# Fewer and planned unread products at the start, value loads on a second DMA queue, and operands read into other places

## The chip, the cores and the metric

The kernel runs on one core of a Trainium2 chip. A core has five engines with a program each: TensorE (PE, matrix products), VectorE (DVE), ScalarE (ACT), GpSimd (POOL) and SyncE (SP), which in this kernel only issues DMA. They wait for one another through semaphores. The metric is the device time of one execution in microseconds (us); lower is better.

## The reference

Attention in chunks of 32 rows, each of which looks at 8 memory keys and at the keys from 16 rows before the chunk to 8 rows after it (64 in all), and then two feed-forward layers of 512 by 2048, all in float32:

```python
for c in range(nc):                       # 24 chunks of 32, 4 batches x 8 heads, head_dim 64
    q_c = q[:, :, c_start:c_end]
    k_full = np.concatenate([mem_k, k[:, :, l_start:r_end]], axis=2)
    v_full = np.concatenate([mem_v, v[:, :, l_start:r_end]], axis=2)
    scores = scale * np.matmul(q_c, k_full.transpose(0, 1, 3, 2))
    a = np.exp(scores - np.max(scores, axis=-1, keepdims=True))
    a = a / (np.sum(a, axis=-1, keepdims=True) + 1e-09)
    out[:, :, c_start:c_end] = np.matmul(a, v_full)
...
h = x @ w_in                              # x: 3072 x 512, w_in: 512 x 2048
g = h * np.clip(h + 3.0, 0.0, 6.0) / 6.0
x = g @ w_out                             # 2048 x 512
...
h = x @ w_in2
x = np.maximum(0.01 * h, h) @ w_out2
```

## The kernel before, in words

**The products.** Nearly all of the work is the four large matrix products. They run on TensorE in a float32 form of reduced precision, with each operand split into a high and a low part; a product of one 128-wide slice of the hidden layer with 512 rows is 12 matmuls of 128x512 (`h<-xh,w` eight times and `h<-xl,w` four times at L998, and `y<-g,w` twelve times at L1047). Later blocks of rows go in pairs, by a scheme with seven products in place of eight (L1322, L1490), whose sums of operands and results are made on ACT, DVE and POOL (`x_pair` reads the operands, L1126; L341 and L344 are the helpers that record copies, casts and two-operand operations, whatever they are for).

**The weights** arrive as 64-bit words (L393, 512 KB each, 32 per layer), are turned into float32 by ACT (L396) and DVE (L400, L404, L408), and are then split into their two parts (L341, L344).

**The attention** is cut into units. The first two (`unit(0, 0)` and `unit(0, 1)`, with the PSUM banks `at` and `ab`) and two half units (banks `h` and `ac`) come before any product; the others are threaded between the products. A unit loads queries and keys (`qk`), copies keys into windows (L341 on ACT, DVE or POOL), makes scores on PE (L544; L811 for half units), takes maxima (DVE, L561), exponentials (ACT, L568 and L580; L845), sums and norms (L594, L598), transposes on PE (L602; L866), copies the transposed rows back (`take_p`, ACT L341), multiplies with the values on PE (L622 and L634; L882) and hands rows on as operand `xh`, `xl` of the products or to the DRAM tensor `attended`. The values of a unit come in two tiles of six DMAs each: L502 four times (56x3x128, 84 KB) and L504 twice (8x6x128), all on SP's queue. Up to the unit whose scores start at 201 us they land in places of the pool `w`; the values, queries and keys of the four later units, and the operands `x` of the pairs, lie in places of the smaller pool `a`.

**The order.** Nobody wrote the order of instructions by hand. Every step is a task with an engine, a cost in ns and what it depends on, and `schedule` (a list scheduler with a model of DMA lanes, of the instruction queue of PE and of buffers) writes each engine's program from them; the engines then run their programs strictly in order. A change of any cost, and any new task, can therefore reorder all five programs.

**The unread products.** `warm` adds tasks that multiply the identity `ident` with itself into a bank that nobody reads (L461). They stand at fixed places: ahead of the first scores and behind each of the following steps of the four early units, first 512 columns wide, later 256. A float32 matmul of this kind, as those of the attention, is two instructions on PE in the trace: `x48` in the order is `x96` in the trace. The transposes are one each.

## Time and profile before

| | |
|---|---|
| median of 3 runs | 1046.41 us (1045.3 to 1048.34) |
| profiled execution | 1046.62 us |
| its span, from the first to the last instruction | 1044.8 us |
| PE busy | 1029.5 us, 99% of the span |
| DVE, ACT, POOL busy | 856.0, 694.8 and 23.9 us |
| mean granted TensorE clock | 0.998 |
| chain that ended last | PE 85%, DMA 6%, DVE 4%, ACT 2% |

The profiled execution is 0.2 us above the median, and 1.8 us of it lie outside the span. Times in rows are microseconds from the span's start. In a row of the timeline, "x17" is the number of instructions merged into it, and what stands in brackets is how long the engine had been idle before it and what ended that; "issue" is a wait for nothing that the profile shows.

### The profile page before, as it was taken

The numbers are of one execution on the slowest core, as the hardware profiler recorded it, in microseconds if no ns is written. First come the engines' busy times: TensorE is split into PE (matmuls) and PEld (weight loads), VectorE is DVE, ScalarE is ACT, GpSimd is POOL, SyncE is SP. The second block draws the span as 40 slices with busy tenths as digits, with TensorE's granted clock in tenths as the row PEclk, the third lists the DMA queues.
The fourth block names the chain that finished last, engine by engine and source line by source line (L and its number), as shares of the span: only waits on it lengthen the run. The fifth ranks groups of instructions, "written<-read, shape, count | busy, mean of one in ns | idle before, by whom it ended". The sixth has DMA issues, their size and how long they took to land.

```text
span 1044.8 us, 20156 instructions
## 1 busy us (share of the span) xinstructions
PE 1029.5 (99%) x7476; PEld 846.7 (81%) x7476; DVE 856.0 (82%) x1422; ACT 694.8 (67%) x1478; POOL 23.9 (2%) x31
## 2 busy tenths in 40 slices
PE   7999999999999999999999999999999999999998
PEld 4788888877888888888888888888888888888887
DVE  6995897578998778699999898999476998566775
ACT  4886776555988554576786576776565874666753
POOL 3010000000000000000000000000000000000000
PEclk9999999999999999999999999999999999999999
DMA  9989787776888888664647884446342554432451
GB/s 259 298 237 323 256 286 236 247 256 215 276 288 292 292 279 278 245 217 127 212 135 268 291 286 162 147 158 218 117 167 81 177 194 153 169 114 95 148 181 61
DMA packets 127315, 220.50 MB, mean 211 GB/s; under 512 B 12528, under 2 KB 76016, under 8 KB 127216
## 3 DMA queue, kind: packets, MB, share of 16 engines
q1 hardware_dynamic: 127216, 219.20, 63.2%
q8 instruction: 59, 0.97, 0.4%
q14 instruction: 40, 0.33, 0.1%
HBM read 156.24 MB, written 62.91 MB: 210 GB/s over the span
## 4 chain that ended last, share of the span: by engine, by line
PE 85%; DMA 6%; DVE 4%; ACT 2%; SPq 2%; issue 1%; DVEq 0%; ACTq 0%
PE y L1322 17%; PE y L1490 12%; PE h L1322 11%; PE y L1047 10%; PE h L1490 8%; PE hx L1322 8%; PE hx L1490 8%; PE h L998 3%; PE h L1047 2%; DMA w<-in_raw 2%; DMA kept1i<-ys 1%; DMA a<-in_raw 1%; PE at L634 1%; DMA half<-ys 1%; PE at L544 1%
## 5 line engine op out<-in xcount | busy, mean ns | idle before, releaser
L344 DVE TENSOR_TENSOR w<-w 128x512 fp32r<-128x512 f32 (+2 forms) x393 | 323.3, 858 | 29.0 <-ACT w L341 28.4
L341 ACT CAST w<-w 128x512 fp32r<-128x512 f32 (+1 forms) x290 | 223.7, 805 | 12.5 <-DMA w<-floats 3.9
L1047 PE MATMUL y<-g,w 128*128 128x512 f32 (+1 forms) x540 | 124.9, 375 | 1.5 <-ACT g L341 0.6
L1322 PE MATMUL y<-w 128*128 128x512 f32 x516 | 124.2, 389 | 0.0
L1322 PEld LDWEIGHTS y<-w 128*128 128x128 f32 x516 | 96.7, 188 | 20.1
L1047 PEld LDWEIGHTS y<-g,w 128*128 128x128 f32 x540 | 94.0, 188 | 19.9 <-ACT g L341 1.4
L1490 PE MATMUL y<-w 128*128 128x512 f32 x384 | 90.3, 389 | 0.0
L341 ACT CAST g<-w 128x512 fp32r<-128x512 f32 x80 | 49.7, 623 | 58.3 <-PE y L1490 22.5
L1490 PEld LDWEIGHTS y<-w 128*128 128x128 f32 x384 | 72.1, 188 | 15.0
L1296 ACT ACTIVATE w<-w 128x512 f32<-128x512 f32 x72 | 45.3, 633 | 43.9 <-DVE w L1289 21.5
L998 PE MATMUL h<-xh,w 128*128 128x512 f32 (+1 forms) x288 | 66.0, 370 | 0.0
L344 DVE TENSOR_TENSOR g<-w,g 128x512 fp32r<-128x512 f32 x80 | 54.4, 689 | 11.5 <-ACT g L341 11.4
L1490 PE MATMUL h<-w 128*128 128x512 f32 x264 | 62.1, 389 | 0.0
L1322 PE MATMUL h<-xl,w 128*128 128x512 f32 x240 | 58.3, 391 | 1.2 <-ACT xl L341 1.2
L1490 PE MATMUL hx<-w 128*128 128x512 f32 x252 | 59.2, 389 | 0.0
L1490 PEld LDWEIGHTS h<-w 128*128 128x128 f32 x264 | 49.5, 188 | 10.3
L998 PEld LDWEIGHTS h<-xh,w 128*128 128x128 f32 x288 | 49.7, 188 | 9.0
L1490 PEld LDWEIGHTS hx<-w 128*128 128x128 f32 x252 | 47.3, 188 | 9.8
L1322 PEld LDWEIGHTS h<-xl,w 128*128 128x128 f32 x240 | 44.8, 188 | 11.3 <-ACT xl L341 1.6
L1322 PE MATMUL y<-xh,w 128*128 128x512 f32 x216 | 51.9, 389 | 0.0
L1367 DVE TENSOR_TENSOR w<-y,w 128x512 f32<-128x512 f32 x35 | 23.9, 687 | 29.9 <-PE y L1322 27.1
L1322 PEld LDWEIGHTS y<-xh,w 128*128 128x128 f32 x216 | 40.5, 188 | 8.5
(242 smaller groups left out, 1847.7 us busy)
## 6 DMA issues: line engine op xcount, KB each, us to landing
w<-kept2i SPq DMA_DIRECT2D x42, 512.0 KB
w<-kept2o SPq DMA_DIRECT2D x42, 512.0 KB
w<-kept1i SPq DMA_DIRECT2D x28, 512.0 KB
a<-in_raw SPq DMA_DIRECT2D x20, 448.0 KB
w<-in_w1i SPq DMA_DIRECT2D x16, 512.0 KB
w<-in_w1o SPq DMA_DIRECT2D x16, 512.0 KB
w<-in_w2i SPq DMA_DIRECT2D x16, 512.0 KB
w<-in_w2o SPq DMA_DIRECT2D x16, 512.0 KB
```

Of the source, the lines that this page charges most:

```text
L341: nc.scalar.copy(out, in_) if e == "ACT" else engine(e).tensor_copy(out=out, in_=in_)
L344: engine(e).tensor_tensor(out=out, in0=a, in1=b, op=ALU.subtract)
L544: nc.tensor.matmul(ps.t[h * CHUNK:(h + 1) * CHUNK, par, i * W:(i + 1) * W], qk[h // 2].t[r, gp, (h % 2) * G + c * CHUNK:(h % 2) * G + (c + ...
L634: nc.tensor.matmul(pv.t[(h % 2) * D:(h % 2 + 1) * D, par, (h // 2) * 2 * G + i * CHUNK:(h // 2) * 2 * G + (i + 1) * CHUNK], v[h // 2].t[r, ...
L998: nc.tensor.matmul(h.t[:, o:o + n], w.t[:, 1 if p == 1 else 0, k * 128:(k + 1) * 128], x[:, k, c0:c0 + n], start=(p == 0 and k == 0 and o ...
L1047: nc.tensor.matmul(bank(banks[d])[:, c0:c0 + n], w.t[:, 1 if p == 1 else 0, d * 128:(d + 1) * 128], g.t[:, 1 if p == 2 else 0, at:at + n], ...
L1296: return add(lambda e: nc.scalar.activation(out=at(), in_=at(), func=AF.Prelu, alpha=0.01), {"ACT": act(N)}, key, after=[after], uses=uses)
L1322: nc.tensor.matmul(bank(to), wt(l, o)[:, kt * 128:(kt + 1) * 128].bitcast(F32R), operand(p, name, 1 if q == 2 else 0, kt).bitcast(F32R), s ...
L1367: done[2] = add(lambda e: nc.vector.tensor_tensor(out=half_of(x, 0), in0=bank(bb), in1=ut.t[:, 0], op=ALU.add), low, key, after=[k, done[1 ...
L1490: nc.tensor.matmul(bank(to[d]), wt(1 if q == 1 else 0, o)[:, d * 128:(d + 1) * 128].bitcast(F32R), g.t[:, 1 if q == 2 else 0], start=(fres ...
```

## The change

1. `warm` and its fixed places are gone. `schedule` itself puts in an unread product (`filler`, L483 in the changed kernel) wherever it finds PE without a task before the first large product, as long as a bank is open for it (`opens` and `closes` on the attention's steps say when): 128 columns wide before the first scores, 256 after.
2. The values of units 4 and later (`by_pool`) are issued by GpSimd's queue, 96 DMAs in eight units, 12 a unit; the loads ahead of them stay on SP.
3. Weights 2 to 23 get a `hold`: GpSimd copies one element of the weight two before, once that has landed, into the new weight's place, and the load waits for that copy. So at most two of these loads are under way.
4. The operands of the first pair (`x_pair`, p < -1) are read into places of `w`, not of `a`.
5. The windows of the second early unit are copied by ACT and not by DVE.
6. Costs and due times of the planner: cheaper value loads, another model of when a load has landed and of the instruction queue of PE, no safety margin before 20 us.

```diff
-STARTS, LANDS, SURE = 1900.0, 500.0, 1500.0
-HELD, FETCHED, FETCH, STALL = 447, 256, 5000.0, 250.0
+STARTS, LANDS, SURE, SOONER, MOST = 1900.0, 250.0, (0.0, 1500.0), 20000.0, 8000.0
+HELD, FETCHED, ASKS, FETCH, STALL = 447, 256, (256, 400), 2500.0, 250.0
+FIRST, LATER, FIRST_TILL = (128, 430.0), (256, 450.0), 3800.0
...
                 if pick is None:
+                    if e == "PE" and not progress and spots and (begun or now < FIRST_TILL):
+                        cols, took = LATER if begun else FIRST
+                        filler(spots[0], cols)
...
                     continue
...
+        if hold:
+            before, landed = hold
+
+            def follow(e):
+                nc.gpsimd.tensor_copy(out=make(t, ([128, 512, 2], U32))[:1, 0, :1].bitcast(F32), in_=before.t[:1, 0, :1].bitcast(F32))
+
+            k = add(follow, {"POOL": 100.0}, early, after=[*after, landed], allocs=[t], uses=[before])
+            k = add(load, {"SP": dma(524288, 380.0)}, early, after=[k], uses=[t])
...
+        by_pool = j >= 4 and not plain
...
-                        nc.sync.dma_start(out=v[i].t[par * D + NMEM:(par + 1) * D, g], in_=there)
+                        (nc.gpsimd if by_pool else nc.sync).dma_start(out=v[i].t[par * D + NMEM:(par + 1) * D, g], in_=there)
...
-        t = [add(windows(i), ({"DVE": 850.0} if i or quad else {"ACT": 1050.0}) if j == 0 else {"ACT": 1050.0}, key - 30, after=[l1[i]], allocs=[kw[i]], uses=[qk[i]]) for i in range(2)]
+        t = [add(windows(i), ({"DVE": 850.0} if i and not quad else {"ACT": 1050.0}) if j == 0 else {"ACT": 1050.0}, key - 30, after=[l1[i]], allocs=[kw[i]], uses=[qk[i]]) for i in range(2)]
...
-        src = {n: Buf("a") for n in ("b11", "b12", "b21", "b22")}
+        src = {n: Buf("w" if p < -1 else "a") for n in ("b11", "b12", "b21", "b22")}
...
-    warm(2)
-    warm(1, marks["s", 0, 0])
-    warm(2, marks["s", 0, 1])
...
-    for m, n in ((("s", 1, 1, 0), 2), (("t", 0, 0), 3), (("t", 0, 1), 3), (("t", 1, 1, 0), 2), (("v", 1, 0, 0), 2)):
-        warm(n, marks[m], home)
```

Lines move by 16 to 22 between the two kernels: L461 becomes L483, L602 L624, L622 L644, L634 L656, L811 L833, L866 L888, L882 L904, L998 L1019, L1047 L1068, L1322 L1343; L393 becomes L409, L491 L511, L502 L524, L504 L526, L1126 L1147.

**PE at the start.** PE's program of the kernel before, from the third group of scores (half unit, bank `h`) on; ahead of these rows stand 2, 1 and 2 unread products of 512 columns and the scores of `at` and `ab`, 48 matmuls each:

```order
L811 MATMUL h<-w 32x64 x24
L461 MATMUL ac<-ident 128x512
L811 MATMUL ac<-w 32x64 x24
L602 MATMUL at<-ident,w 128x128 x6
L461 MATMUL ac<-ident 128x256 x5
L622 MATMUL at<-w 64x32 x48
L602 MATMUL ab<-ident,w 128x128 x6
L461 MATMUL ac<-ident 128x256 x3
L866 MATMUL h<-ident,w 128x128 x3
L866 MATMUL ac<-ident,w 128x128 x3
L622 MATMUL ab<-w 64x32 x48
L461 MATMUL ac<-ident 128x256 x2
```

The changed kernel at the same place; ahead of it stand 9 unread products of 128 columns, the scores of `at`, 4 of 256 columns, the scores of `ab` and 3 of 256 columns:

```order
L483 MATMUL ac<-ident 128x256 x3
L624 MATMUL at<-ident,w 128x128 x6
L833 MATMUL h<-w 32x64 x24
L833 MATMUL ac<-w 32x64 x24
L644 MATMUL at<-w 64x32 x48
L624 MATMUL ab<-ident,w 128x128 x6
L888 MATMUL h<-ident,w 128x128 x3
L483 MATMUL h<-ident 128x256 x2
L888 MATMUL ac<-ident,w 128x128 x3
L483 MATMUL h<-ident 128x256
L644 MATMUL ab<-w 64x32 x48
L904 MATMUL h<-w 64x32 x24
```

The transposes of `at` have moved ahead of the half units' scores, the values of `at` stand right behind these, and of the unread products between the scores of `h` and the first values none is left (one of 512 columns and five of 256 before).

**PE in the last unit whose values lie in `w`** (its scores are the first row of each fence). The kernel before:

```order
L544 MATMUL at<-w,a 32x64 x48
L998 MATMUL h<-xl,w 128x512 x4
L1047 MATMUL y<-g,w 128x512 x12
L998 MATMUL h<-xh,w 128x512 x8
L998 MATMUL h<-xl,w 128x512 x4
L602 MATMUL at<-ident,w 128x128 x6
L1047 MATMUL y<-g,w 128x512 x8
L634 MATMUL at<-w 64x32 x48
```

The changed kernel:

```order
L566 MATMUL at<-w,a 32x64 x48
L1068 MATMUL y<-g,w 128x512 x8
L1019 MATMUL h<-xh,w 128x512 x8
L1019 MATMUL h<-xl,w 128x512 x4
L1068 MATMUL y<-g,w 128x512 x12
L1019 MATMUL h<-xh,w 128x512 x8
L624 MATMUL at<-ident,w 128x128 x6
L1019 MATMUL h<-xl,w 128x512 x4
L1068 MATMUL y<-g,w 128x512 x12
L656 MATMUL at<-w 64x32 x48
```

Between scores and transposes stood 28 matmuls of 128x512 before, and now 40.

**SP at the first pair's operands.** SP's program of the kernel before: the last of the first pair's eight reads (`a<-attended`), with other transfers around it (the value loads of the first unit with values in `a`, L502 and L504, follow a few rows on):

```order
L1219 DMA kept2i<-wm 128x256 x2
L1126 DMA a<-attended 128x512
L1219 DMA kept2i<-wm 128x256
L1088 DMA spill<-ys 128x512
L1084 DMA ys<-half 128x512
L1088 DMA spill<-ys 128x512
L1265 DMA w<-kept1i 128x1024
```

The changed kernel, where all eight operands are read into `w`:

```order
L1240 DMA kept1i<-ys 128x256 x4
L1147 DMA w<-attended 128x512 x7
L409 DMA w<-in_w2i 128x1024
L1147 DMA w<-attended 128x512
L409 DMA w<-in_w2i 128x1024
L1240 DMA kept2i<-st 128x256
```

The reads have moved together and up, and the value loads are gone from here: L524 and L526 stand on POOL, whose program behind the norm of the last but one unit with values in `w` is nothing but these loads, four and two per tile.

In the last four units, whose values lie in `a`, 72 matmuls of 128x512 now stand between the scores and the values of the unit, where it was 50 to 56. POOL, which did the norms (L598) of these four units before, does none of theirs now; DVE has them.

## Rows read from the trace of the kernel before

**Rows 1.** Windows: us, then busy time (instructions) of PE, PEld, DVE, ACT, POOL; clock; DMA

```profile
0.00:36.60 36.60, 29.05 (x679) 18.83 (x679) 25.66 (x66) 19.20 (x74) 11.14 (x23) 0.95 0.88 256
36.60:260.00 223.40, 219.15 (x2635) 182.04 (x2630) 177.35 (x342) 154.61 (x474) 6.28 (x4) 1.00 0.80 262
260.00:1044.80 784.80, 781.26 (x4171) 645.87 (x4169) 652.98 (x1014) 521.03 (x931) 6.50 (x4) 1.00 0.58 194
15.00:18.00 3.00, 2.94 (x65) 1.20 (x53) 1.78 (x6) 1.36 (x10) 0.25 (x1) 0.50 1.06 270
```

**Rows 2.** Waits of PE: us in total, times, longest

```profile
PE ac L461 <- ACT w L845: 2.0, 1, 2.0
...
PE h L1322 <- ACT xl L341: 1.2, 1, 1.2
```

**Rows 3.** Timeline of PE up to the first large product: start, duration

```profile
12.75 0.35 PE L811 MATMUL h<-w 64*32 64x64 f32 x17 [0.28 <-POOL w L341]
...
14.80 0.67 PE L811 MATMUL h<-w 64*32 64x64 f32 x29 [1.70 <-issue]
...
24.04 1.78 PE L622 MATMUL at<-w 64*64 64x32 f32 x96
...
28.51 0.95 PE L622 MATMUL ab<-w 64*64 64x32 f32 x45
...
30.21 1.10 PE L622 MATMUL ab<-w 64*64 64x32 f32 x51 [0.76 <-issue]
...
35.31 0.70 PE L882 MATMUL ac<-w 64*64 64x32 f32 x28 [0.47 <-issue]
...
36.60 2.11 PE L998 MATMUL h<-xh,w 128*128 128x512 f32 x8
```

**Rows 4.** Timeline of ACT in the same stretch

```profile
19.38 0.78 ACT L341 COPY w<-at 128x768 f32<-128x768 f32 x1
...
21.04 0.32 ACT L845 ACTIVATE w<-ac,mx 128x64 f32<-128x64 f32 x1 [0.88 <-PE ac L461]
...
26.77 0.84 ACT L341 COPY w<-ab 128x768 f32<-128x768 f32 x1
```

**Rows 5.** Timeline of PE, last unit with values in `w`

```profile
201.44 1.17 PE L544 MATMUL at<-w,a 64*32 64x64 f32 x96
...
210.15 0.84 PE L602 MATMUL at<-ident,w 128*128 128x128 f32 x6 [0.94 <-DVE w L598]
```

**Rows 6.** Timeline of SP, last operand read of the first pair

```profile
247.52 0.32 SPq L1126 DMA_DIRECT2D a<-attended  x1
```

**Rows 7.** Timeline of DVE in the following microseconds

```profile
252.26 0.69 DVE L1080 SCALAR_TENSOR_TENSOR ys<-y,ys 128x512 f32<-128x512 f32 x1 [2.79 <-PE y L1047]
```

**Rows 8.** Timeline of ACT there

```profile
255.01 0.62 ACT L341 CAST xl<-w 128x512 fp32r<-128x512 f32 x1 [1.38 <-DVE w L344]
```

**Rows 9.** Timeline of POOL: copies of arrived values, and a norm

```profile
23.41 3.52 POOL L341 COPY w<-w 8x768 f32<-8x768 f32 x4 [0.45 <-DMA w<-in_raw]
...
113.36 1.65 POOL L598 TENSOR_TENSOR w<-w,mx 128x768 f32<-128x768 f32 x1 [38.85 <-DVE mx L594]
```

**Rows 10.** Line L502, value loads into `a`: ns min/median/max, first and last start

```profile
L502 SPq DMA_DIRECT2D a<-in_raw x32: 315/400/1880, 272.6 to 356.5; - x32
```

**Rows 11.** Timeline of SP, value loads of a half unit

```profile
17.96 1.92 SPq L778 DMA_DIRECT2D w<-in_raw  x2
```

**Rows 12.** Timeline of PE, first unit with values in `a`

```profile
271.35 1.17 PE L544 MATMUL at<-a 64*32 64x64 f32 x96
...
276.23 2.88 PE L1322 MATMUL y<-w 128*128 128x512 f32 x12
...
285.61 1.62 PE L634 MATMUL at<-a 64*64 64x32 f32 x96
```

**Rows 13.** Timeline of DVE during that norm

```profile
113.60 1.96 DVE L408 SCALAR_TENSOR_TENSOR st<-w,st 128x512 uint32<-128x512 uint32 x1
```

**Rows 14.** Windows with line L400 alone: us, DVE busy (instructions); clock; DMA

```profile
250.00:370.00 120.00, 5.07 (x10) 1.00 0.82 271
```

More of the change, by code (lines that the diff above doesn't have):

```diff
@@ L68, with __init__ @@
 class Task:
-    def __init__(self, fn, opts, key, after=(), allocs=(), uses=(), moe=False, issues=1, late=0, loads=False, ins=8):
-        self.late, self.loads, self.ins = late, loads, ins
+    def __init__(self, fn, opts, key, after=(), allocs=(), uses=(), moe=False, issues=1, late=0, loads=False, ins=8, opens=None, closes=()):
+        self.late, self.loads, self.ins, self.opens, self.closes = late, loads, ins, opens, closes
         self.fn, self.opts, self.key, self.moe, self.issues = fn, opts, key, moe, issues
@@ L120, in feed @@
                 held, comes = held + FETCHED, None
-            if comes is None and used >= held - FETCHED:
-                comes = at + FETCH
+            if comes is None and used >= held - ASKS[at > 45000]:
+                comes = min(max(at, max((y for x, y in queued if x <= at), default=0.0)) + FETCH, at + MOST)
             if used >= held:
@@ L170, in finish @@
             if not t.left:
-                push(now + (MARGIN if "PE" in t.opts and not t.moe else 0.0), "ready", t)
+                push(now + (MARGIN if "PE" in t.opts and not t.moe and now > SOONER else 0.0), "ready", t)
     for t in tasks:
@@ L223, in schedule @@
                 if pick is None:
+                    if e == "PE" and not progress and spots and (begun or now < FIRST_TILL):
+                        cols, took = LATER if begun else FIRST
+                        filler(spots[0], cols)
+                        fill = Task(None, {"PE": took}, 0, ins=4)
+                        end, queue = feed(now, fill)
+                        free[e] = end
+                        push(end, "free", None)
                     continue
                 pick.taken = True
+                begun = begun or e == "PE"
+                for b in pick.closes:
+                    if b in spots:
+                        spots.remove(b)
                 for b in pick.allocs:
@@ L386, in tile_attn_moe_moe2, with decode @@
     wbuf, wtask = {}, {}
-    def decode(src, f, key, early=None, after=(), place="wm", gate=(), late=0, own=True, split=None):
+    def decode(src, f, key, early=None, after=(), place="wm", gate=(), late=0, own=True, split=None, hold=()):
         t, m = Buf("w"), Buf(place)
         def load(e):
-            nc.sync.dma_start(out=make(t, ([128, 512, 2], U32)).rearrange("p w s -> p (w s)"), in_=src[f])
+            nc.sync.dma_start(out=made_as(t, [128, 512, 2], U32).rearrange("p w s -> p (w s)"), in_=src[f])
         def scaled(e):
@@ L1407, in seven, with made_as @@
                 put(r, add(lambda e: nc.scalar.activation(out=make(r), in_=bank(ba), func=AF.Prelu, alpha=0.01), {"ACT": act(N, 50.0)}, key, after=[k, done[7]], allocs=[r], uses=[ba]))
-    def made_as(b, shape):
-        return b.t if b.t is not None else make(b, (shape, F32))
+    def made_as(b, shape, kind=F32):
+        return b.t if b.t is not None else make(b, (shape, kind))
     def waiting_parts(j, f):
@@ L1583, in tile_attn_moe_moe2 @@
             alone_ = f >= KF // 2
-            parts = decode(src, f, at - 8, early[i] if i < len(early) else min(at - 38, 6 * i - 40), splits[before:before + 1] if before >= 0 else (), "ys" if i % 2 else ("wm", "st")[f // 2 % 2] if alone_ else "wm", gate=behind if 3 <= i < 6 else (), own=alone_, split=which if alone_ else None)
+            parts = decode(src, f, at - 8, early[i] if i < len(early) else min(at - 38, 6 * i - 40), splits[before:before + 1] if before >= 0 else (), "ys" if i % 2 else ("wm", "st")[f // 2 % 2] if alone_ else "wm", gate=behind if 3 <= i < 6 else (), own=alone_, split=which if alone_ else None, hold=arrivals[i - 2] if 2 <= i < 24 else ())
             if alone_:
@@ L1634, in tile_attn_moe_moe2 @@
         constants()
-        schedule(tasks, places, ends)
+        schedule(tasks, places, ends, filler, [begun_at])
 def kernel(**inputs):
```

62 lines of the change are left out of this document (31 added, 31 removed).

## The prediction

> **What bounds the kernel now.** I first divide the span into windows [rows 1]. From 260 us on, PE is busy for 781.3 of 784.8 us, and what is missing is about the 3.5 us behind its last product: nothing can be gained there except by doing less, and the change leaves the products alone. Between 36.6 and 260 us 4.3 us are missing, in a few holes. Up to 36.6 us, where the first large product starts, PE is busy for 29.1 us, but part of that is unread products. So there are two places to gain: an earlier first product, which moves all that follows, and the holes. There is one way to lose much: a new hole after 36.6, since every microsecond for which PE waits there is one of the total.
>
> The waits of PE [rows 2] and its first 37 us [rows 3] show what holds the start. Three waits have "issue" as their reason: 1.70 us up to 14.80, 0.76 up to 30.21 and 0.47 up to 35.31. Counting PE's instructions (twice the order's number for float32 products, once for transposes) puts them after 221, 475 and 602 of them, so 254 and 127 apart: multiples of 127. I read this as PE's own program arriving in batches of about 127 products. The boundary between the first two falls a third into the values of `at`, at 24.04 + 0.6 = 24.6, and passes without a wait.
>
> Then there is a wait by order. The transposed rows of `at` were copied back at 19.38 + 0.78 = 20.16 [rows 4], but their values start at 24.04: ahead of them stand unread products into bank `ac`, which wait 2.0 us for exponentials that read `ac` (from 21.04).
>
> The two holes in the middle that the change touches: transposes wait 0.94 us for a norm at 210.15 [rows 5], and at 255.7 PE waits 1.2 us for the cast of `xl` [rows 2].
>
> **The start, worked out.** In the changed order the instructions up to the transposes of `at` are 18 + 96 + 8 + 96 + 6 = 224, so the first boundary (221) stands just ahead of the transposes and not inside the scores of `h`. It is the same batch, so 14.80 again. The next (348) falls 22 instructions into the values of `at`, 475 falls 35 into the values of `ab`, 602 falls 18 into those of `ac`; behind that stands as much as before (30 instructions and 48 scores where it was 28 and 48), so the first product follows 36.60 - 35.31 = 1.3 us later, as now.
>
> When does a batch come? From the first use of one to the next being there it took 30.21 - 24.6 = 5.6 and 35.31 - 30.21 = 5.1 us. For `at` that gives 14.80 + 5.1 to 5.6 = 20 to 20.4; its values end near 21.8 instead of 25.8. For `ab` ACT decides: its copy of `ab` (26.77) stands behind six exponentials of `ac` (1.9 us, not before 21 by the scores), two casts and four short ones (some 2.3 us). If the exponentials start at 21.0 the copy is at 25.2, if a weight's scaling and the maxima ahead of them make them 1.5 us later it is at 26.7. The values of `ab` then start 0.9 us later, at 26.1 to 27.6 (28.51 now), their boundary is 0.6 behind that, the last batch 5.1 to 5.6 later, at 31.8 to 33.8, and the first product at 33.1 to 35.1. I take 34.1, a **gain of 2.5 us**.
>
> Bounds: batches that follow one another at 5.1 us whether used or not allow 14.8 + 15.3 + 1.3 = 31.4, and the copies on ACT some 32: gain 4.5. If each takes half of the time from 14.80 to 30.21, which is 7.7, the first product is at 14.8 + 23.1 + 1.3 = 39.2: a loss of 2.6. The unread products that go cost nothing in themselves, since they fill waits. But the granted clock was at 0.50, the lower of its two levels (1.2 GHz), from 15 to 18 us, after the wait of 1.70 [rows 1]; with fewer fillers there the same may last some microseconds longer. Of 3 us at half speed 1.5 are lost, of which a waiting PE hides most; up to 1 us is inside these bounds.
>
> The Trainium skill ("Runtime: NRT & Kernel Launch", "Instruction fetch mechanics") says that programs come in blocks of 256 instructions, which fits 127 products with a weight load each, and that crossing to the next is mostly hidden. The first the trace bears out, the second not: 2.9 us of waits here. By that sentence alone the batches would not count and the first product would be near 32, the bound above.
>
> **The holes.** At 210 the transposes stand 28 matmuls behind the scores (201.44 to 210.15 less 0.94 of waiting [rows 5]), and the chain of maxima, exponentials and norm took 0.94 longer than that. The changed order puts 40 there; at 0.23 us each this adds 2.8 us. The hole of **0.9 us goes**. At 255 the last of the eight operand reads was issued only at 247.52 [rows 6]; the DVE operations on it stand behind one that waits for PE until 252.26 [rows 7], and the cast on ACT that waits for them starts at 255.01 [rows 8]. Now all eight are read together into places of `w`, ahead of the unit's loads, so **1.2 us go**. The other holes between 36.6 and 260 (together 2.1 us) I leave as they are.
>
> **The weights held in pairs.** A product of 12 matmuls takes about 2.7 us and uses one weight; with two under way each may take 5.4 us from issue to landing. The SP queue can stall behind a POOL copy. Early, POOL is busy with copies of arrived values (3.52 us for four from 23.41 [rows 9]), so a hold can be that late, till 26.9 with the first product at 34. I count nothing, and 1.5 us as the upper bound.
>
> **GpSimd's DMA issues.** This is the cost that the trace doesn't show: there is no DMA on POOL. A load costs SP 0.40 us [rows 10]. POOL's own steps cost 0.88 us each for copies of 8 rows and 1.65 for a norm [rows 9]. So 0.4 to 1.65 us per issue; I take 1.0, near the copies, which are like it in that POOL handles some tens of rows.
>
> How much is hidden? Take the four last units, where `a` has few places. The values can be loaded when the windows are copied, so about from the scores on. Before, scores to values took 285.61 - 271.35 = 14.3 us with 54 matmuls between [rows 12]; now there are 72, which adds 18 x 0.23 = 4.1: 18.4 us. From the last issue to use takes 23.41 - 19.88 = 3.5 us, by a half unit's loads (17.96 + 1.92 [rows 11], used by POOL at 23.41 [rows 9]). That leaves 14.9 us for 12 issues: **1.2 us each are free**. Above that each 0.1 us costs 1.2 us per unit, 4.8 over four units. At 1.0 the term is zero; at 1.65 it is 12 x 0.41 x 4 = 20 us. The norms that moved from POOL to DVE leave POOL nothing else there. That SP is relieved of 96 issues (38 us at 0.40) gains nothing by itself: no wait of PE ended on a value load.
>
> **The sum.** 2.5 + 0.9 + 1.2 = 4.6 us off 1046.62, the profiled execution's own time, is 1042.0; the median of before is 0.2 lower, so **1041.8 us**.
>
> **Rivals.**
> - *GpSimd's queue is too slow* (slower). Place: the values of the four last units, behind 12 issues. It decides from 1.2 us per issue and eats the whole gain at 1.34. At 1.45 it costs 12 and the time is 1054. For it: the norm's 1.65. Against: the copies' 0.88.
> - *DVE and POOL lock one another.* While POOL did a norm from 113.36 to 115.01, a DVE operation that began at 113.60 lasted 1.96 us [rows 13], where one of its size took 0.69 [rows 7]: one waited for the other. If each issue has to wait for DVE operations of that kind, it is longer by their share. For the only line that I know to run faster than the rest, L400, that is 5.07 of 120 us [rows 14], 4%: 1.0 becomes 1.04 and nothing happens. If it holds for most of DVE's operations (83% busy from 260 us [rows 1]), an issue takes several times as long and the rival above is certain: 1060 or more. The Trainium skill warns of just this ("SBUF — State Buffer", "SBUF: two separate sides"): during DVE's two-port operations GpSimd can't write the descriptors of its DMAs, and the same transfer from SP's queue is free of it. The trace shows the lock with a norm; with a DMA no run here does.
> - *The start gains nothing.* The batches come as late as they can, or ACT's chain is 1.5 us later still: only the holes remain, 1044.5.
> - *The start gains all*: 4.5 + 2.1, and 1 us of the other holes: 1039.
>
> **How the numbers follow.** A measurement here tells about 0.3%, 3.1 us, from no change. Forecast (hidden issues, start gains 1 to 4 us): 0.52. Start gains all: 0.08. Start gains nothing: 0.12, within 0.3%. Issues between 1.2 and 1.4 us: 0.10, time 1043 to 1051, two thirds of it within 0.3%. Issues dearer or locked: 0.14, slower. A new wait by the held weights or another reordering that eats the gain: 0.04. Faster 0.58, within 0.3% 0.25, slower 0.17. The likeliest case alone is 1040 to 1043.5; the range reaches to the full gain at the start, 1038.5, and to issues of 1.4 us, 1041.8 + 0.18 x 48 = 1050.5.
>
> **What would show it.** The first `h<-xh,w` starts near 34 us. Issue waits of PE stand ahead of the transposes of `at`, in the values of `at` and in those of `ac`. No wait above 0.3 us is left at about 205 and 250 us. POOL's queue shows its DMA issues at about 1 us, and no value product waits on them. I am wrong if PE waits ahead of `at<-a` values (L656) in the last four units, if the issues are over 1.2 us, or if the first product starts after 36.

## The result, and the profile after

The changed kernel takes 1056.88 us (median of 6 executions, 1054.55 to 1057.73); the kernel before, run beside it, takes 1046.76 (6 executions, 1044.45 to 1048.73). The ratio is 1.0094, with a 95% interval of 1.0081 to 1.0107: **slower by 0.9%**, where 1041.8 had been forecast. The profiled execution took 1054.55 us with a span of 1052.7, which is 7.9 more than the span before.

The windows of the kernel after, with the columns of [rows 1]; the first three answer to the first three there:

```profile
0.00:35.46 35.46, 26.58 (x680) 22.26 (x680) 24.87 (x61) 21.50 (x82) 12.58 (x27) 0.84 0.88 255
35.46:260.00 224.54, 216.59 (x2699) 180.55 (x2695) 175.79 (x337) 154.45 (x477) 45.83 (x72) 0.98 0.84 263
260.00:1052.70 792.70, 787.69 (x4106) 650.93 (x4104) 655.31 (x1021) 520.53 (x928) 30.18 (x48) 1.00 0.58 192
...
35.00:40.00 5.00, 5.00 (x53) 3.99 (x35) 4.43 (x15) 4.12 (x17) 0.56 (x2) 0.75 0.82 235
60.00:65.00 5.00, 5.00 (x48) 4.01 (x42) 5.00 (x11) 4.49 (x13) 0.35 (x1) 0.66 1.09 249
125.00:130.00 5.00, 4.13 (x53) 3.87 (x54) 3.87 (x9) 2.53 (x14) 0.83 (x1) 1.00 0.90 278
200.00:205.00 5.00, 4.58 (x75) 3.68 (x76) 1.30 (x4) 2.25 (x16) 0.11 (x1) 0.66 0.98 337
...
205.00:215.00 10.00, 10.00 (x49) 8.33 (x48) 3.23 (x6) 4.73 (x15) 0.00 (x0) 1.00 0.06 20
245.00:260.00 15.00, 15.00 (x158) 12.23 (x158) 13.40 (x23) 8.41 (x22) 0.21 (x1) 1.00 0.69 220
```

With [rows 1] these give the whole account of the 7.9 us:

- The first large product starts at 35.46 instead of 36.60: 1.1 gained, where 2.5 was forecast.
- Behind it PE is idle for 224.54 - 216.59 + 792.70 - 787.69 = 13.0 us; before, the same sum was 4.25 + 3.54 = 7.8. That is **5.2 us of new waits**.
- Behind it PE is busy for 216.59 + 787.69 = 1004.3 us, with 6,805 instructions; before, it was 1000.4 with 6,806. The same work takes **3.9 us longer**. The clock column says why: two windows stand at 0.66, each behind a hole, and the one in which the large products begin, from 35 to 40 us, stands at 0.75 (1.00 in the kernel before).

-1.1 + 5.2 + 3.9 = 8.0, and the spans differ by 7.9. The last two rows of the fence show that the two holes that the change was expected to close, at 210 and 255, are closed: PE is busy all the time there.

PE's waits after (us in total, times, longest); those of the first product's stretch are left out:

```profile
PE at L566 <- issue: 3.9, 3, 1.8
PE at L916 <- ACT w L357: 3.4, 2, 2.6
...
PE y L1343 <- ACT w L357: 0.7, 1, 0.7
PE at L656 <- DMA a<-in_raw: 0.6, 1, 0.6
```

Two are new and large. L566 makes scores, and its three waits have the reason that was read as "PE's own program has not arrived"; in the kernel before, such waits mattered only in the first 36 us. L916 is the values of a half unit, behind a copy on ACT. PE's timeline around the largest of each:

```profile
55.72 1.09 PE L1019 MATMUL h<-xl,w 128*128 128x512 f32 x4
59.43 1.14 PE L916 MATMUL at<-w 64*64 64x32 f32 x48 [2.62 <-ACT w L357]
...
60.49 3.91 PE L1068 MATMUL y<-g,w 128*128 128x512 f32 x10
...
198.13 0.45 PE L566 MATMUL at<-w,a 64*32 64x64 f32 x31
200.42 0.86 PE L566 MATMUL at<-w,a 64*32 64x64 f32 x65 [1.84 <-issue]
...
201.21 3.68 PE L1068 MATMUL y<-g,w 128*128 128x512 f32 x8
```

The row behind each hole is as telling as the hole. Eight matmuls of this size take 2.11 us [rows 3]; at 201.21 they take 3.68, and ten at 60.49 take 3.91 where 2.6 would be full speed. So the hole of 1.84 costs 1.84 + 1.6, and the one of 2.62 costs 2.62 + 1.3. The rest of the 3.9 us is at the start, below.

The count of PE's instructions says what the waits for "issue" are. In a window from 0 to the end of a wait, PE's number is how many instructions stood ahead of it; here up to the largest of the three waits:

```profile
0.00:200.42 200.42, 183.58 (x2876) 153.74 (x2877) 160.63 (x326) 142.68 (x478) 58.20 (x98) 0.96 0.90 274
```

The three waits stand behind 1862, 2622 and 2876 instructions. The last batch of the start ends after 599 (602 in the kernel before), and from there on that is 10, 16 and 18 batches of some 126.4 instructions, the size of a batch at the start: these waits are ends of batches too. In another order (e5, below) PE waits behind 1863, 2623 and 2875. From the first use of a batch until the next one was there it took 5.2, 4.6 and 5.7 us (an estimate, by the same counts). The batch was used up in 3.8 to 4.0 us of that, since 118 of its 126 instructions are small ones of values and scores.

What was late at 59.43? ACT's timeline, and below it SP's:

```profile
57.83 0.66 ACT L412 ACTIVATE wm<-w 128x512 f32<-128x512 f32 x1 [2.86 <-DMA w<-in_w1i]
...
58.91 0.47 ACT L357 COPY w<-at 128x384 f32<-128x384 f32 x1
```

```profile
52.83 0.35 SPq L409 DMA_DIRECT2D w<-in_w1i  x1
```

SP of the kernel before, at the same load:

```profile
41.84 0.42 SPq L393 DMA_DIRECT2D w<-in_w1i  x1
```

ACT stands for 2.86 us in front of a weight that has not landed. The copy for which PE waits (58.91) has nothing to do with that weight; it is merely behind it in ACT's program. SP issued the weight at 52.83, 5.0 us before. This is one of the weights held in pairs; it is the eleventh load of a weight, and in the kernel before the eleventh was issued at 41.84.

On GpSimd's queue, line L524 (its loads into `a`; ns min/median/max), and then POOL's timeline in the last unit:

```profile
L524 POOL DMA_DIRECT2D a<-in_raw x32: 657/662/666, 259.8 to 367.0; - x32
...
DMA to landing us min/median/max: 2.6/5.7/9.3
```

```profile
358.42 1.32 POOL L524 DMA_DIRECT2D a<-in_raw  x2
363.07 0.58 POOL L526 DMA_DIRECT2D a<-in_raw  x1 [3.33 <-DMA a<-in_raw]
366.35 1.32 POOL L524 DMA_DIRECT2D a<-in_raw  x2 [2.70 <-issue]
```

An issue takes 0.66 us, below the 1.0 of the forecast and with hardly any spread. But the queue stands for 3.33 us until an earlier load of its own has landed, and then 2.70 more; a load lands 5.7 us after its issue (in the median) where 3.5 had been estimated. By the count, the load for which the queue waits is the eighth before it: the one issued at 363.07 is the ninth from 354.64 on. The model in `schedule` gives a queue eight lanes as well (`LANES = 8`). The wait of 0.6 us in the list (L656, values in `a`) is what reaches PE of that.

PE's timeline at the start, which answers to [rows 3]:

```profile
14.26 1.44 PE L483 MATMUL ac<-ident 128*128 128x256 f32 x3 [2.68 <-issue]
...
18.10 0.62 PE L644 MATMUL at<-w 64*64 64x32 f32 x21
20.75 2.49 PE L644 MATMUL at<-w 64*64 64x32 f32 x75 [2.04 <-issue]
...
28.25 0.52 PE L888 MATMUL ac<-ident,w 128*128 128x128 f32 x3 [1.19 <-DVE w L884]
...
29.14 1.78 PE L644 MATMUL ab<-w 64*64 64x32 f32 x96
...
33.13 0.72 PE L904 MATMUL ac<-w 64*64 64x32 f32 x33 [1.19 <-issue]
34.08 1.45 PE L833 MATMUL at<-w 64*32 64x64 f32 x48 [0.22 <-ACT w L357]
35.46 3.03 PE L1019 MATMUL h<-xh,w 128*128 128x512 f32 x8
```

The batches of PE's program come near to where they were forecast: the first at 14.26 (14.80), the next after 21 instructions of the values of `at` (22), at 20.75 (20 to 20.4), the last at 33.13 (31.8 to 33.8). Behind that the score products of 34.08 take 1.45 us, where the same products take 0.73 in another kernel below (e8, at 36.09), and from the last boundary to the first product it is 2.3 us instead of 1.3. The first eight large matmuls then take 3.03 us where they took 2.11 [rows 3], so that 0.9 of the 1.1 us gained are lost again at once.

Nor is 1.1 us more than two executions of one program differ by. The run f1 below has PE's program of the kernel before word for word, and GpSimd issues its first value load only behind 130 us; its PE timeline:

```profile
35.13 2.11 PE L998 MATMUL h<-xh,w 128*128 128x512 f32 x8
```

That is 1.5 us earlier than the 36.60 of the kernel before. With the changed kernel's PE program, the first product starts at 36.20 in e1 and at 36.16 in e2.

### The profile page after: what moved, and what is told of

Same layout as the page of the kernel before. It is cut to its first block, busy times and chain, and to the rows that moved or that the text cites. A ratio compares the mean times of both kernels' runs of the same rounds, so it can differ in the third digit from the quotient of the medians.

```text
span 1052.7 us, 20313 instructions
## 1 busy us (share of the span) xinstructions
PE 1030.9 (98%) x7478; PEld 853.7 (81%) x7478; DVE 856.0 (81%) x1416; ACT 696.5 (66%) x1487; POOL 88.6 (8%) x146
## 4 chain that ended last, share of the span: by engine, by line
PE 87%; DMA 8%; DVE 2%; issue 1%; ACT 1%; SPq 1%; POOL 0%; POOLq 0%; DVEq 0%; ACTq 0%
PE y L1343 16%; PE y L1511 12%; PE y L1068 12%; PE h L1343 10%; PE h L1511 8%; PE hx L1511 8%; PE hx L1343 7%; PE h L1019 6%; DMA w<-in_raw 3%; PE h L1068 2%; PE at L656 2%; DMA w<-in_w1i 2%; DMA a<-in_raw 1%; PE at L566 1%; DMA kept2o<-wm 1%
## 5 line engine op out<-in xcount | busy, mean ns | idle before, releaser
L360 DVE TENSOR_TENSOR w<-w 128x512 fp32r<-128x512 f32 (+2 forms) x407 | 333.0, 857 | 30.9 <-ACT w L357 30.3
L357 ACT CAST w<-w 128x512 fp32r<-128x512 f32 (+1 forms) x296 | 226.4, 799 | 12.6 <-PE hx L1511 3.9
L1068 PE MATMUL y<-g,w 128*128 128x512 f32 (+1 forms) x540 | 126.9, 381 | 0.5 <-DVE g L360 0.5
L1343 PE MATMUL y<-w 128*128 128x512 f32 x516 | 124.9, 391 | 0.7 <-ACT w L357 0.7
L1343 PEld LDWEIGHTS y<-w 128*128 128x128 f32 x516 | 96.5, 188 | 21.1 <-ACT w L357 1.1
L1068 PEld LDWEIGHTS y<-g,w 128*128 128x128 f32 x540 | 96.4, 192 | 19.4 <-DVE g L360 1.2
L1019 PE MATMUL h<-xh,w 128*128 128x512 f32 (+1 forms) x288 | 67.2, 375 | 0.0
L1343 PE MATMUL h<-xl,w 128*128 128x512 f32 x240 | 58.0, 390 | 0.0
L1019 PEld LDWEIGHTS h<-xh,w 128*128 128x128 f32 x288 | 50.5, 192 | 9.2 <-issue 0.2
L1343 PEld LDWEIGHTS h<-xl,w 128*128 128x128 f32 x240 | 44.9, 188 | 9.2
L1343 PE MATMUL y<-xh,w 128*128 128x512 f32 x216 | 51.9, 389 | 0.0
L1343 PEld LDWEIGHTS y<-xh,w 128*128 128x128 f32 x216 | 40.6, 188 | 8.4
```

The costliest lines, as they stand in the source:

```text
L357: nc.scalar.copy(out, in_) if e == "ACT" else engine(e).tensor_copy(out=out, in_=in_)
L360: engine(e).tensor_tensor(out=out, in0=a, in1=b, op=ALU.subtract)
L1019: nc.tensor.matmul(h.t[:, o:o + n], w.t[:, 1 if p == 1 else 0, k * 128:(k + 1) * 128], x[:, k, c0:c0 + n], start=(p == 0 and k == 0 and o ...
L1068: nc.tensor.matmul(bank(banks[d])[:, c0:c0 + n], w.t[:, 1 if p == 1 else 0, d * 128:(d + 1) * 128], g.t[:, 1 if p == 2 else 0, at:at + n], ...
L1343: nc.tensor.matmul(bank(to), wt(l, o)[:, kt * 128:(kt + 1) * 128].bitcast(F32R), operand(p, name, 1 if q == 2 else 0, kt).bitcast(F32R), s ...
```

## The experiments

All ratios are to the kernel before, run on the same chip, with a 95% interval. Lines in the diffs are of the kernel that the experiment starts from. Of the four suspects (the weights' order and GpSimd's copies that hold it, the value loads on GpSimd, the planner's new model of PE's instruction queue, the placing of the unread products) most runs undo one or add one alone.

**e1: without GpSimd's one-element copies.** The tasks stay in the plan, so every other engine's program is that of the changed kernel.

```diff
-                nc.gpsimd.tensor_copy(out=make(t, ([128, 512, 2], U32))[:1, 0, :1].bitcast(F32), in_=before.t[:1, 0, :1].bitcast(F32))
+                make(t, ([128, 512, 2], U32))
```

> The changed kernel without GpSimd's one-element copies of the held weights, so that a weight's load waits only for its place; every other instruction stands where it stood. Theory A (the hold makes a weight late at 57.8 us, and the 2.6 us hole behind it also lowers the granted clock): the wait of the values at 59.4 us goes, the clock of 60 to 65 us is 1.00 and not 0.66, and the time falls by 3.5 to 4.5 us, to about 1052.5. Rival B (the transfers themselves are too slow there, whatever starts them): with more loads under way they share the same rate, the hole stays above 1.5 us and the time within 1.5 us of 1056.9. The issue waits at 126, 181 and 200 us stay under both.

1056.9 us, 1.0092 [1.0078, 1.0107]: the same as the changed kernel, as rival B had it. The hole is there as before; ACT waits 3.29 us at 59.86 for a weight that SP issued at 53.17. PE's timeline, and two pieces of the chain of work (start, time from issue to landing):

```profile
61.46 1.87 PE L916 MATMUL at<-w 64*64 64x32 f32 x48 [2.82 <-ACT w L357]
```

```profile
48.70 4.38 DMA w<-in_w1i
...
53.17 6.61 DMA w<-in_w1i
```

So the copies are not the cause. But this run does not take the wait away: SP issues the weight at 53.17, 0.1 us after the weight two before has landed (48.70 + 4.38), as if it were held. Six value loads stand between these two weights, so the earlier one is also the eighth load before on SP's queue. In this order the queue waits where the copy had waited. What is left of the hold is the order into which the planner puts the weights' loads on SP because of it.

**e2: the value loads issued by SP**, while the plan still has them on GpSimd. PE's, DVE's and ACT's programs are those of the changed kernel.

```diff
-                        (nc.gpsimd if by_pool else nc.sync).dma_start(out=v[i].t[par * D + NMEM:(par + 1) * D, g], in_=there)
+                        nc.sync.dma_start(out=v[i].t[par * D + NMEM:(par + 1) * D, g], in_=there)
```

> The changed kernel with the 96 value loads issued by SP at the place where the planner put them for GpSimd; PE, DVE and ACT keep their programs word for word. Theory A (the issue waits before scores come from PE's own program arriving too slowly for values and scores that stand close together): the waits of about 1.4, 0.7 and 1.8 us at 126, 181 and 200 us stay, and the time changes by less than 2 us. Rival B (GpSimd's DMA delays PE's instruction transfers, or DVE): the three waits go and the time falls by 4 to 6 us. Rival C (SP's queue is then the late one): new waits of the value products and a longer time.

1051.2 us, 1.0047 [1.0029, 1.0065], half of the loss. Neither theory fits as it was written: two of the three waits stay (theory A), and the time falls as rival B had it. PE's timeline at the three places where it waited for "issue":

```profile
124.45 0.44 PE L566 MATMUL at<-w,a 64*32 64x64 f32 x26 [1.35 <-issue]
...
179.03 0.81 PE L566 MATMUL at<-w,a 64*32 64x64 f32 x60 [0.47 <-issue]
...
196.47 1.17 PE L566 MATMUL at<-w,a 64*32 64x64 f32 x96
```

With the same PE program, the third wait is gone (it is 1.44 us in e1, with GpSimd's queue), and with it the slow clock (1.00 from 190 to 210, PE busy 20.00 of 20); the waits at 372 and 643 are gone too: 1.84 + 1.6 + 0.6 + 0.7 = 4.7 us, against 1.0094 - 1.0047 = 0.47%, 4.9 us. (The profiled execution, 1047.11 us, was the fastest of six, up to 1054.52; the hole at 59 is missing in it, and its weight was issued at 50.09 instead of 52.83. The profile therefore doesn't stand for the median there, and that 4.7 comes so near to 4.9 is no proof of the single terms.)

**e3: the former model of PE's instruction queue in the planner** (a batch is asked for 256 instructions ahead and comes 5 us later, whatever DMA traffic there is).

```diff
-HELD, FETCHED, ASKS, FETCH, STALL = 447, 256, (256, 400), 2500.0, 250.0
+HELD, FETCHED, ASKS, FETCH, STALL = 447, 256, (256, 400), 5000.0, 250.0
...
-            if comes is None and used >= held - ASKS[at > 45000]:
-                comes = min(max(at, max((y for x, y in queued if x <= at), default=0.0)) + FETCH, at + MOST)
+            if comes is None and used >= held - ASKS[0]:
+                comes = at + FETCH
```

> The changed kernel with the planner's former model of PE's instruction transfers (asked for 256 instructions ahead, 5 us each), everything else as changed; the planner reorders freely. Theory A (the new model lets the planner put values and scores too close together): the issue waits behind 100 us are below 0.5 us in sum (3.9 now), no clock drop at 200 us, and the time is 5 us lower, about 1052, with the hole at 59 us still there. Rival B (the waits come from elsewhere): they stay above 2.5 us in sum.

1048.54 us, 1.0014 [1.0002, 1.0026]: nearly all of the loss is gone, although hold and GpSimd's queue stay. The first product starts at 31.03, and no scores wait for "issue". The planner has changed the start as well as the scores: of the 5.9 us between the two profiled spans 4.4 are the earlier first product. Two holes behind weights remain (59.34 and 75.30), with a clock of 0.69 and 0.67 in their windows:

```profile
PE h L1019 <- ACT w L357: 4.0, 2, 2.3
```

**e4: e1 and e3 together.**

> Both edits together: no hold copies, and the former model of instruction transfers. If the two causes are separate and are all of the loss, about 1047 (the two gains added, 9 to 10 us), that is the time of before within 0.3%; if they are all of it and the start's gain of 1.1 us and the two removed holes of 2.1 us are kept, 1044. If something else costs time too, above 1049.

1048.88 us, 1.0022 [1.0005, 1.0039], not to be told from e3: again taking out the copies is worth nothing.

**e5: planned without the hold**; the weights' order on SP is then that of before.

```diff
-hold=arrivals[i - 2] if 2 <= i < 24 else ()
+hold=()
```

> The changed kernel whose planner knows nothing of the hold, so that the weights stand on SP's queue as in the kernel before (13 of them in its first 49 rows, where the changed kernel has 9). Theory A (the hold's order on SP, not its copies, makes the weight late that PE waits for at 59 us): no wait of PE above 0.5 us between 45 and 100 us, clock 1.00 there, 4 us faster than the changed kernel, about 1052.5; the issue waits before scores (3.9 us) stay. Rival B (the many value loads in the same stretch make it late): the wait is still there.

1054.77 us, 1.0083 [1.0060, 1.0105]; this can't be told from the changed kernel. The windows and PE's timeline show why:

```profile
45.00:100.00 55.00, 54.75 (x761) 45.40 (x760) 44.02 (x86) 44.67 (x140) 3.06 (x2) 1.00 0.91 290
```

```profile
201.78 1.19 PE L566 MATMUL at<-w,a 64*32 64x64 f32 x65 [2.55 <-issue]
```

The weights' hole is gone, as theory A expected of their order, but the time stays: four waits for "issue" add up to 6.1 us (4.8 at the scores, 1.3 at `h`) where they were 3.9, two of them with half clock behind, and the first product starts at 36.55.

**e6: e5 with the former queue model; e7: e6 with the values back on SP, in the plan too** (`by_pool = False`).

> As the run before, and with the planner's former model of PE's instruction transfers as well. Theory A (these two edits are all of the loss): no issue wait above 0.5 us behind 40 us, no weight wait, 1044 to 1046, faster than or the same as before. Rival B (the loads on GpSimd's queue also cost): still 1048 or more, with waits on values or on the clock behind 120 us.

> As the run before, and the values of all units on SP's queue in the planner too. What is left of the change is the planned unread products at the start, the operands in the places of weights and the smaller costs. Theory A (GpSimd's queue neither gains nor costs): within 1.5 us of the run before. Rival B (it costs): 2 to 4 us faster than the run before. If the left parts gain what the prediction said of them, about 1043.

e6: 1048.98 us, 1.0031 [1.0017, 1.0046], without waits for "issue" behind the first product (30.05), but with a new hole of 3.11 us at 101.30 behind a cast on ACT and one of 2.23 at 211.65. e7: 1045.0 us, 0.9990 [0.9979, 1.0001]. So with neither hold nor the new model, GpSimd's queue costs 0.41%, 4.3 us, together with the other order that the planner writes for it; rival B came true. The 1043 that the prediction's gains would have left is missed.

**e8: the kernel before with the operands in `w`, and nothing else.**

```diff
-        src = {n: Buf("a") for n in ("b11", "b12", "b21", "b22")}
+        src = {n: Buf("w" if p < -1 else "a") for n in ("b11", "b12", "b21", "b22")}
```

> The kernel before with one edit of the change alone: the first pair's operands are read into places of w. The step of the prediction: the wait of 1.2 us at 255 us goes, and the time falls by about that, to 1045.3; the holes at 112 and 210 us may move, since the planner reorders what comes behind. Rival (the places of w are needed by weights): a new wait for weights behind 250 us, the same time or more.

1043.92 us, **0.9979 [0.9967, 0.9991]: faster than both kernels.** The eight reads stand together on SP (timeline), done by 225.3, 22 us ahead of the last one before [rows 6], and the hole at 255 is gone:

```profile
221.49 3.79 SPq L1126 DMA_DIRECT2D w<-attended x8
```

**e9: e8 without the five unread products of 256 columns into `ac`**, which stand ahead of the first values; **e10: without all twelve behind the early steps.**

> The kernel before with the operands in w, less the five unread products of 256 columns into bank ac that stand ahead of the first values and wait for ACT; every other instruction stands where it stood. Theory A (the order of the start was the loss, as the prediction worked it out): the values of at start at 20 to 21 us (24.0 before), the first large product 1 to 3 us earlier, at 33.6 to 35.6, and the time falls by as much, to 1041 to 1043. Rival B (the instruction transfers or ACT set the start, and the unread products only fill): first product within 0.7 us of 36.7. Rival C (without them the granted clock falls to its lower level and takes the gain back): clock below 0.8 in two or more of the 5 us windows from 20 to 45 us, time not lower.

> As the run before, without any of the twelve unread products of 256 columns of the start; the six of 512 columns stay. Theory A: the clock is not hurt, and the first product starts no later than there. Rival C (they hold the clock up): clock at the lower level for 5 us or more between 20 and 45 us and the first product 1 us or more later than in the run before.

1044.79 us, 0.9987 [0.9977, 0.9997], and 1044.87 us, 0.9988 [0.9979, 0.9996]: neither better nor, for certain, worse than e8. PE's timeline in e9:

```profile
21.40 1.79 PE L622 MATMUL at<-w 64*64 64x32 f32 x96 [0.94 <-ACT w L341]
...
33.72 0.58 PE L882 MATMUL ac<-w 64*64 64x32 f32 x19 [1.79 <-issue]
36.34 1.46 PE L811 MATMUL at<-w 64*32 64x64 f32 x48 [2.04 <-ACT w L341]
37.72 1.65 PE L998 MATMUL h<-xh,w 128*128 128x512 f32 x3
```

The values of `at` start 1.4 us earlier than in e8 (22.77), the first product 1.0 us later (36.75 in e8). Clock and waits further on took it back: 0.50 from 35 to 40 us, where e8 has 1.00. In e10 the first product starts at 36.47, with a clock of 0.55 and 0.50 in the two windows from 30 to 40 us.

**e11: e7 with the planner's former costs and margins**, so that of the change only the operands and the planned unread products are left; **e12: e7 with the former cost of a value load** (`RATE_V` 300).

> The kernel before with two edits of the change alone: the operands in w, and the planned unread products in place of the fixed ones, with the former costs, due times and instruction model, no hold, nothing on GpSimd's queue. Theory A (planned fillers gain at the start what the prediction said, 2.5 us): first product near 34 and 1041.5. Rival B (the gain at the start in other runs came with the planner's other costs): first product at 36 or later and no faster than the kernel with the operands alone, 1044.

> As the run e7 (no hold, former instruction model, all values on SP), with the planner's former rate for value loads too. If the three holes of e7 near 100 us (0.9, 1.7 and 0.5 us, and a low clock behind them) came from loads planned too early or too late, they are below 1 us in sum, the first product still starts before 33 us, and the time is 1042. If not, 1045 as e7.

e11: 1049.35 us, 1.0028 [1.0015, 1.0042], which is 0.49% above e8: planned unread products with the former costs lose 5 us (first product at 37.72, half clock from 30 to 40). Rival B of its expectation came true. e12: 1044.76 us, 0.9990 [0.9977, 1.0003], as e7, with the first product at 30.28.

The last three add one suspect alone to the kernel before.

**f1: the value loads issued by GpSimd**, not planned for; PE's, DVE's and ACT's programs stay.

```diff
-                        nc.sync.dma_start(out=v[i].t[par * D + NMEM:(par + 1) * D, g], in_=there)
+                        (nc.gpsimd if j >= 4 and not plain else nc.sync).dma_start(out=v[i].t[par * D + NMEM:(par + 1) * D, g], in_=there)
```

> The kernel before with the 96 later value loads issued by GpSimd, in the planner's old places; PE, DVE and ACT keep their programs word for word. Theory A (GpSimd's queue does harm only where PE's instructions are dense, as in the changed order): 1046 to 1048, within 1.5 us of before, no issue wait behind 40 us. Rival B (it costs by itself): 1049 or more, with waits of PE on values, on instructions or on norms behind 120 us.

1060.92 us, 1.0127 [1.0112, 1.0142], the slowest of all: rival B. PE's waits, and POOL's timeline:

```profile
PE at L602 <- POOL a L598: 7.5, 3, 4.3
PE at L634 <- DMA a<-in_raw: 2.5, 2, 1.5
```

```profile
365.61 0.58 POOL L504 DMA_DIRECT2D a<-in_raw  x1 [2.25 <-DMA a<-in_raw]
368.76 1.32 POOL L502 DMA_DIRECT2D a<-in_raw  x2 [2.57 <-issue]
370.09 0.59 POOL L504 DMA_DIRECT2D a<-in_raw  x1
370.69 1.48 POOL L598 TENSOR_TENSOR a<-a,mx 128x768 f32<-128x768 f32 x1
```

Here POOL still has the norms. The norm starts when the last load is issued, and the loads ahead of it stand for 2.25 and 2.57 us. What it reads is ready at 365.13 (DVE, L594), 5.6 us before: the queue's two waits are 4.8 of them. In this unit it is these waits, more than the issues, that hold PE.

**f2: the new queue model alone; f3: the hold alone.**

> The kernel before with the new planner model of PE's instruction transfers alone; the planner reorders freely. Theory A (this model puts values and scores too close together): two or more issue waits of over 0.5 us behind 100 us, the clock lower behind the longest of them, 1049 to 1052. Rival B (it needs the rest of the change): no such waits, 1045 to 1048.

> The kernel before with the hold of weights 2 to 23 alone; the planner reorders freely. Theory A (the hold's order makes weights late when the value loads come between): a wait of PE of over 1 us between 45 and 100 us that ends on a weight's decoding, a low clock behind it, 1049 to 1051. Rival B (it only does so behind the earlier start): 1045 to 1048, no such wait.

f2: 1045.7 us, 0.9998 [0.9986, 1.0009]. Waits for "issue" of 0.8 and 1.5 us do appear (at L1050 and at scores, L547), the clock stays at 1.00 around the second, and there is no net loss. f3: 1052.43 us, 1.0056 [1.0041, 1.0071]. The new model alone does nothing to the time, the hold alone costs 5.9 us. Of the 6.8 us between the profiled spans of f3 and of the kernel before, 1.7 are a later first product (38.27), 2.6 new waits and 2.6 a longer time for the same products. f3's ACT and then PE show the changed kernel's hole once more:

```profile
60.73 0.66 ACT L396 ACTIVATE wm<-w 128x512 f32<-128x512 f32 x1 [2.83 <-DMA w<-in_w1i]
```

```profile
62.81 1.14 PE L905 MATMUL at<-w 64*64 64x32 f32 x48 [2.40 <-ACT w L341]
```

## Why the prediction was wrong

**The step that failed first** is the one that ends "I count nothing, and 1.5 us as the upper bound", on the weights held in pairs. Alone it costs 5.9 us (f3), in the changed kernel a hole of 2.62 us and 1.3 of slow clock behind it. I had looked for what stalls behind the hold on SP, and sized it by POOL's copies; e1 shows that these don't matter. What matters is the order that the planner makes of it: SP issues the weight 11 us later than before (52.83 instead of 41.84), and with 5.0 us from issue to landing it is late for ACT, whose program has other work queued behind it, a copy for PE among that. "Each may take 5.4 us" was the limit that the step itself had given, and the weight kept it (4.9 us); but it was issued only 6.3 us after the weight two before it (46.54), with six value loads between them on the queue. In e5, without the hold in the plan, the hole is gone. I had not asked what stands behind the weight's first reader on ACT.

**"At 1.0 the term is zero"**, on GpSimd's issues, was right in its price (0.66 instead of 1.0) and wrong in its conclusion. The term was issues times price; it left out that a queue waits for its own earlier loads, by the count for the eighth before (3.33 us in one place), and that a load lands 5.7 us after its issue. Loads on GpSimd cost 4.9 us in the changed kernel (e2), 4.3 with the planner's order for it, without the hold and the new model (e6 against e7), and 0.6 us of the first are PE's direct wait for values, which the forecast had named as a sign of being wrong.

**The instruction batches were counted only up to the first product.** The count goes on behind it, and with the prediction's own 5.1 to 5.6 us from one batch to the next it would have told of these waits (5.2, 4.6 and 5.7 measured). "The other holes I leave as they are" holds for what is there, not for what the new order makes: scores now stand close behind values (8 matmuls of 128x512 between them ahead of the scores at 198.13, where before it was 16 ahead of those at 201.44), and three waits of 3.9 us in all come of it. That the planned order is at fault shows in e3 and e6, planned with the former model, which have no such waits at the scores (e11, with the former model too, has one of 1.6); that GpSimd's queue has a share shows in e2, where the wait at 200 goes with PE's program unchanged, while e1 keeps 1.44 us of it. Each of these is one profiled execution; how the two act together is not shown. The DMA share from 195 to 200 us is 1.01 in the changed kernel and 0.87 in e2, so a full DMA may hold PE's program back there, but this is only argued.

**Each hole was priced at its own length.** Behind the first product the slower products cost 3.9 us on top of the 5.2 of new waits: 1.6 and 1.3 behind two holes and 0.9 at the first products.

**The start** was right in that batches of the program decide it, and too large: 1.1 us instead of 2.5, less than two executions differ by, and 0.9 of it lost in the first products. The batches came within 0.6 us of their forecast or inside its range, the last one by luck: from the first use of a batch to the next it took 6.5 us (14.26 to 20.75) and 3.4 (from the first behind 475 instructions, at 29.7, to 33.13), where 5.1 to 5.6 was counted with. Nor did ACT decide for `ab`: its values started at 29.14 instead of 26.1 to 27.6, because the transposes of `ac` ahead of them waited 1.19 us for DVE. What was mis-sized besides is the stretch behind the last batch, 2.3 us instead of 1.3; the "up to 1 us" for the clock was in the bounds but not in the sum. What kept the start from gaining more is the order planned with the new queue model: with the former one e3, e4, e6, e7 and e12 have the first product at 30.05 to 34.42, with the new one the changed kernel, e1, e2 and e5 at 35.46 to 36.55 (e11, with the other former costs as well, at 37.72). e9 and e10 show that fewer unread products alone don't do it: taken out, they made the values earlier and the first product not by more than executions differ.

**Right** were the holes at 210 and 255, with 0.9 and 1.2 us; e8 has the second alone and gains 2.2 (0.9 to 3.5 by its interval).

**The rivals.** GpSimd's queue was too slow, though not by issues above 1.2 us, the point from which I had it decide. The lock of DVE and POOL has nothing for it in the issues: the 32 into `a` lie between 657 and 666 ns, of those into `w` the longest took 863. The Trainium skill ("SBUF — State Buffer", "SBUF: two separate sides") speaks of descriptors that are written late; whether some of the 5.7 us to the landing is of that kind no run here separates. The case that came true, the held weights or another reordering, had been given 0.04.

By ratios, the parts alone on the kernel before come to +0.56% (hold), +1.27% (GpSimd, not planned for), -0.02% (queue model) and -0.21% (operands). Taken out of the changed kernel they are worth nothing that can be told (hold), 0.47% (GpSimd) and 0.80% (queue model). They don't add up in either direction, since most of them (not f1 and e2) let the planner write another order. That is also what stays open: the size of a single part holds only in the order in which it was measured, and each hole is read from one profiled execution. The windows on ACT (part 5) and the costs of part 6 other than the queue model and the rate of value loads have no run of their own; e7 holds them all and is no slower than the kernel before.

## What to carry to other kernels

Where a planner writes the order, a new constraint on a load must be followed to the load's first reader and to everything that is queued behind that reader; the copies that make it may cost nothing (e1) and the order that the planner writes because of it 5.9 us (f3). Where a count explains the waits at the start, carry it on to the end. A queue moved to another engine must be priced by the time that its own waits take, not by issues alone. And try each part of a bundle alone: the smallest, one word in one line (e8), was the only one that gained.

## What the runs showed of the hardware

- **TensorE's clock behind a wait.** Behind the waits of 2.62 and 1.84 us in the changed kernel, 1.77 and 2.55 (e5) and 3.11 (e6), the clock of the window that follows or contains them is 0.50 to 0.66, a mixture of its two levels (1.2 and 2.4 GHz); behind the wait of 1.38 us (changed kernel), that of 1.44 (e1) and that of 1.48 (f2) it is 1.00. A wait of 1.84 us cost 1.6 us more in the products behind it.
- **PE's own program can be late in the middle of a kernel.** The Trainium skill ("Runtime: NRT & Kernel Launch", "Instruction fetch mechanics") calls the crossing from one block to the next mostly hidden. Here it is not: 3.9 us at scores in the changed kernel and 4.8 in e5, at nearly the same counts of PE's instructions (1862, 2622 and 2876; 1863, 2623 and 2875), where small matmuls use up a batch of 126 in about 4 us.
- **A DMA issue on GpSimd** takes 0.66 us (84 KB, 56x3x128) and 0.58 (8x6x128) where SP takes 0.40 for the first [rows 10]. Its loads into `a` (the larger ones) landed after 2.6 to 9.3 us, 5.7 in the median.
